# One transfer for a key tail, a weight half ahead of a read, and a new order in a fused linear-attention and expert kernel

## The chip, the cores and the metric

The kernel runs on one core of one Trainium2 chip. The metric is the device time of one execution in microseconds (us); the engines are TensorE (PE), VectorE (DVE), ScalarE (ACT), GpSimd (POOL) and the queue of SyncE (SP), which issues most transfers.

## The reference

For 8 batches of 8 heads, 576 tokens and 64 columns a head, linear attention is computed and normed, and its 4608 rows of 512 go to one of 16 experts each:

```
kv  = einsum('bhsd,bhse->bhde', k, v)
out = einsum('bhsd,bhde->bhse', q, kv)
x   = out / sqrt(mean(out*out) + 1e-6) * g_norm      # rows of 512
g   = argmax(x @ w_group);  e = argmax(x @ w_expert[g])
y   = softmax weight of g * softmax weight of e * (relu(x @ w1[g, e]) @ w2[g, e])
```

All data are float32. w1 is 512x1024 and w2 is 1024x512 for each expert.

## The kernel before

**Attention.** A batch b has four blocks of 128 tokens and a tail of 64; the tails of two batches (a pair `pb`) share one 128-row piece. So there are 36 tiles of 128 tokens. `load` (L481) brings the main blocks of q, k and v of a batch, 1024 KB each (those of k and v of batch 0 in two halves), and `load_tail` the tails. A tail of v or q is one transfer of 128 partitions (L499). The tail of k goes into `ktail`, a tile of two columns of 512: the rows of the first batch in partitions 0 to 63 of column 0, those of the second in partitions 64 to 127 of column 1, and zeros elsewhere (written once, L488). So k's tail takes two transfers of 64 partitions (L496). `kv_product` (L518) multiplies k and v in four steps of two heads; its fifth term is the tail. `kv_keep`, `kv_transpose`, `kvt_keep`, `router_product` and `router_keep` turn kv into `kvx`, which also holds the router's columns. `o_product` (L564) makes a tile's attention and router logits in one product; ACT copies them out (`o_keep` L569, `logits_keep`, which like the copies of kv is recorded at L507) and squares them (L585); DVE sums the squares (L592).

**Routing.** The tiles form eight groups (6, 5, 5, 4, 4, 5, 4 and 3 tiles). `route` works out each token's expert and row in some 25 small DVE and ACT steps, and POOL then writes each tile with one indirect transfer to `xs` (`put_rows`, L248). After group 1 the busiest expert is chosen (`pick`, which writes `star_idx`); after group 4 (`EARLY`) the place of its first 256 rows is known. When all puts of groups 0 to 4 have landed, `early_region` reads these rows (L273), and `early_weights` loads the expert's four weight halves of 1024 KB (L204), each step behind the one before, the first behind the read. `early_products` scales and transposes the rows (L283, L1182, L1187), multiplies by w1 (L329, eight steps `l1`; ACT's `hhi` L1205 and DVE's `hlo` L1211 behind each) and by w2 (L1234), while the last groups are still being routed.

**The planner.** All of this is a list of steps (engine, cost in us, rank, needs). `give_out` puts them into one written order for each engine: at each turn it takes, on the engine that can start earliest, the step that can start no later than all others of that engine, and among equals the one of lowest rank. "S" stands for the transfers as one resource, START is the time from which a resource is free, and `take` and `give` count 11 slots of a shared pool `big` in which loads and weight pieces live. RANK, ROUTE, FOLD, LOADS, QLOADS and KVS are offsets of the ranks. Idle time of PE in the plan is filled with products of constants (`fill`, tile `warm`, L412). The engines then run their lists in order.

**From the attention to the expert loop.** This stretch is written out by hand. Rows and weights of the second region (r = 0 is what remains of the same expert, r = 1 the next expert) are read; `split_high` (ACT, L227) and `split_low` (DVE, L231) split weights into a high and a low float32r part, and three products (`three`, lines 340, 341 and 345) replace one. The rest r = 0 runs w1 in two halves `hf`, each followed by ACT's relu into `hr` (L1503); `turn(hf)` transposes a half of `hr` on PE (L1475), copies it out on ACT (L1478) and subtracts on DVE (L1479) into `la`; `rest_layer2` needs both. Between them stand the preparations of r = 1: DVE transposes its rows in four pieces (`turned`, L291), ACT scales them (`split_high_x`, L1387) and DVE subtracts (`split_low_x`, L1391).

**The expert loop.** Regions 1 to 15, each layer 1 in eight steps `f` and layer 2 in four steps `d`. In r = 1 the first four steps f also carry one operation each of `quarter_masks` (L1526, L1529, L1531), which mark the rows that count; `indices(1)` follows at f = 4, and POOL scales the rows of r = 2 at f = 0 (L301).

Of the kernel before, what the change touches and what calls it, by code (L numbers as in the profile page):

```python
# [9 lines left out]
F32 = mybir.dt.float32  # L10
# [3 lines left out]
AF = mybir.ActivationFunctionType  # L14
# [21 lines left out]
RANK = {'hl': -4.24, 'wh': -7.85, 'wd': -2246.36, 'ek': 18.16, 'o': 21.14, 'ok': 46.15, 'sq': -11.92, 'red': 65.62, 'w': 51.39, 'wl': -3.08, 'wl2': -1661.94, 'xt': 52.95, 'xs': -122.49, 'l1': 20.45, 'hs': -22.88, 'l2': 25.69, 'lk': -5267.97}  # L36
ROUTE = [1124.11, -2951.7, 3842.35, -3791.13, 68.67, -44.77, -25.9, -5.46]
FOLD = [38.06, 8.5, 5073.95, 6.04, 11066.38, 26.92, -26.59, -20.62]
# [15 lines left out]
START = {"PE": 4.5, "A": 0.5, "D": 0.5, "G": 7.5, "S": 5.8, "R": 9.0, "W": 0.0}  # L54
BIG = 11
CUT = 3

@with_exitstack
def tile_linattn_moe(ctx: ExitStack, tc: tile.TileContext, qm, qt, k, v, router, w1, w2, out):
    nc = tc.nc  # L60
    P = 128
# [311 lines left out]
    with ExitStack() as ph:  # L373
# [96 lines left out]
        def get(*key):  # L470
            return done.get(key)
# [37 lines left out]
        def kv_product(b, pr):  # L509
            if pr == 0:  # L510
                kv["ps"] = ps_k.tile([P, 512], F32, name="kps", tag="psk")
            km, vm, kt, vt = raw["k", b], raw["v", b], tails["k", b // 2], tails["v", b // 2]
# [83 lines left out]
        def attention_steps():  # L596
            for b in range(B):
# [6 lines left out]
                for hi, hs in enumerate(hss):  # L604
                    for x, nm in enumerate(order[:2]):
                        done["load", b, nm, hi] = step(
                            "S", 2.6 / len(hss), f + LOADS[b] + 0.1 * x + 0.3 * hi, [get("load", b, nm, hi - 1)],
# [5 lines left out]
                done["load", b, "q", 0] = step("S", 2.6, f + QLOADS[b], [],  # L613
                                               lambda b=b: load("q", b, everything), take=1)
                if b % 2:
                    done["tail", "q", pb] = step("S", 0.65, f + QLOADS[b] + 0.1,
                                                 [get("o", NT * (pb - 2) + 2 * NJ)] if pb >= 2 else [],
                                                 lambda pb=pb: load_tail("q", pb))
                prev = get("kk", b - 1)
                for pr in range(NP):  # L620
# [3 lines left out]
                                                        done["tail", "k", pb], done["tail", "v", pb]],  # L624
# [6 lines left out]
                prev = step("PE", 0.62, f + RANK["ek"], [prev, get("ek", b - 1)], lambda b=b: kv_transpose(b))  # L631
# [25 lines left out]
        def route(g):  # L657
# [235 lines left out]
            for c in cols:  # L893
# [3 lines left out]
                step("S", 0.7, -100000.0, [prev], lambda: None)  # L897
# [236 lines left out]
        def early_weights():  # L1134
# [3 lines left out]
            for i in range(4):  # L1138
                (wv, rows, cols) = ((w1v, DM, FF // 2), (w2v, FF, DM // 2))[i // 2]

                def f(i=i, wv=wv, rows=rows, cols=cols):
                    if i == 0:
# [4 lines left out]
                               [wt[-1] if wt else st["read"], done["star_idx"]], f,  # L1147
# [129 lines left out]
    with ExitStack() as ph:  # L1277
# [207 lines left out]
        x1, xts = new_x(), []  # L1485
        for hf in range(2):
            ps = ps_h.tile([P, 512], F32, name="ps")
            for c in range(KC):
                if hf == 1 and c == 2:
                    for i in range(2):  # L1490
                        xts.append(turned(1, i))
                        split_high_x(x1[0], xts[i], 1, i)
                    split_low_x(x1, xts[0], 1, 0)
                    turn(0)
                    split_high(w1n[0], 0)
                    xts.append(turned(1, 2))
                    split_low_x(x1, xts[1], 1, 1)
                    split_high_x(x1[0], xts[2], 1, 2)
                    split_low(w1n[0], 0, nc.vector)
                    w1n.append(half_layer(ev, 0, 1))  # L1500
# [215 lines left out]
```

## Time and profile before

| what | value |
|---|---|
| median of 3 runs | 552.08 us (551.42 to 553.18) |
| the profiled execution | 551.76 us |
| its span, first to last instruction | 550.1 us |
| PE busy in the span | 533.0 us, 97% |
| DVE, ACT, POOL busy | 397.7, 281.1, 256.7 us |

The time of the profiled execution is 1.7 us more than its span. A busy PE is not a useful PE: the products of constants at L412 count as busy, so they are looked at apart.

### The profile page before, as it was taken

To read this page: it belongs to the slowest core of one execution; us is meant where nothing else is said; L and a number is where in the kernel's file an instruction comes from. 1 tells how busy PE (TensorE), PEld (TensorE's weight loads), DVE (VectorE), ACT (ScalarE), POOL (GpSimd) and SP (SyncE) were. 2 spreads that over 40 slices of the span, in tenths; PEclk is the share of its full clock that TensorE was granted. 3 is DMA by queue.
4 is the path that set the end of the run, shared out by engine and by line. 5 is a ranking of instruction groups with operands and counts; after the bars stand their busy time and mean duration, and the time that the engine had idled before them with its cause. 6 is when DMAs were issued, how large, how long until landed. Compare 5 with 4: busy or idle time off the path is not lost. (4 is left out here: it accounts for less than half of the span.)

```text
span 550.1 us, 11705 instructions
## 1 busy us (share of the span) xinstructions
PE 533.0 (97%) x4275; PEld 511.0 (93%) x4281; DVE 397.7 (72%) x844; ACT 281.1 (51%) x497; POOL 256.7 (47%) x272
## 2 busy tenths in 40 slices
PE   6999999899999999999999999999999999999995
PEld 3789988689899999999999999999999999999994
DVE  2248999689786786787768677777868777877750
ACT  0377887644653544445354454545453556555440
POOL 5000775452101644737383736455463737355261
PEclk9999999999999999999999999999999999999998
DMA  8999997958987374626756556564738374762010
GB/s 265 377 415 364 415 422 303 337 235 251 326 298 298 85 271 127 242 108 173 276 191 212 199 201 229 168 253 147 278 121 320 87 322 165 262 251 111 9 37 35
DMA packets 44463, 126.30 MB, mean 230 GB/s; under 512 B 6901, under 2 KB 26857, under 8 KB 33396
## 3 DMA queue, kind: packets, MB, share of 16 engines
q1 hardware_dynamic: 36468, 106.01, 53.6%
q0 software_dynamic: 7792, 19.48, 9.5%
q8 instruction: 34, 0.56, 0.4%
q10 hardware_dynamic: 144, 0.04, 0.1%
q14 instruction: 25, 0.20, 0.1%
HBM read 106.04 MB, written 20.58 MB: 230 GB/s over the span
## 5 line engine op out<-in xcount | busy, mean ns | idle before, releaser
L1395 POOL DMA_INDIRECT out_dram<-z,idx x141 | 167.8, 1190 | 169.7 <-DVE idx L1373 131.0
L340 PE MATMUL ps<-xh,whi 128*128 128x364 f32 (+14 forms) x480 | 143.8, 300 | 0.0
L341 PE MATMUL ps<-xl,whi 128*128 128x364 f32 (+14 forms) x480 | 143.8, 300 | 0.0
L345 PE MATMUL ps<-xh,wlo 128*128 128x364 f32 (+14 forms) x480 | 143.7, 299 | 0.0
L345 PE MATMUL psy<-hh,w2l 128*128 128x364 f32 (+13 forms) x448 | 135.0, 301 | 0.4 <-DVE w2l L318 0.4
L340 PE MATMUL psy<-hh,w2h 128*128 128x364 f32 (+13 forms) x448 | 135.1, 302 | 0.0
L341 PE MATMUL psy<-hl,w2h 128*128 128x364 f32 (+13 forms) x448 | 134.8, 301 | 0.0
L231 DVE TENSOR_TENSOR wlo<-wr,whi 128x1024 fp32r<-128x1024 f32 x64 | 94.9, 1486 | 23.2 <-ACT whi L227 23.2
L304 ACT ACTIVATE hh<-ps 128x364 fp32r<-128x364 f32 (+14 forms) x120 | 50.5, 421 | 81.6 <-PE ps L345 79.1
L345 PEld LDWEIGHTS ps<-xh,wlo 128*128 128x128 f32 x480 | 90.6, 189 | 0.0
L340 PEld LDWEIGHTS ps<-xh,whi 128*128 128x128 f32 x480 | 90.6, 189 | 0.0
L341 PEld LDWEIGHTS ps<-xl,whi 128*128 128x128 f32 x480 | 90.5, 188 | 0.0
L314 ACT CAST w2h<-wr 128x1024 fp32r<-128x1024 f32 x60 | 62.6, 1043 | 46.9 <-PE psy L341 46.9
L318 DVE TENSOR_TENSOR w2l<-wr,w2h 128x1024 fp32r<-128x1024 f32 x60 | 73.4, 1224 | 17.8 <-ACT w2h L314 17.3
L345 PEld LDWEIGHTS psy<-hh,w2l 128*128 128x128 f32 x448 | 84.5, 189 | 0.7 <-DVE w2l L318 0.7
L341 PEld LDWEIGHTS psy<-hl,w2h 128*128 128x128 f32 x448 | 84.7, 189 | 0.0
L340 PEld LDWEIGHTS psy<-hh,w2h 128*128 128x128 f32 x448 | 84.6, 189 | 0.0
L305 DVE SCALAR_TENSOR_TENSOR hl<-ps,hh 128x364 fp32r<-128x364 f32 (+14 forms) x120 | 55.7, 464 | 28.0 <-ACT hh L304 27.9
L248 POOL DMA_INDIRECT xs<-xo,keys x36 | 36.1, 1004 | 72.6 <-DVE ohs L756 47.3
L227 ACT CAST whi<-wr 128x1024 fp32r<-128x1024 f32 x64 | 66.4, 1037 | 2.3 <-DMA wr<-in_w_dram 2.3
L1387 ACT ACTIVATE xh<-xt,rw 128x364 fp32r<-128x364 f32 (+14 forms) x60 | 32.6, 545 | 67.6 <-DVE xt L291 67.6
L1597 DVE STREAM_TRANSPOSE z<-psy 128x320 f32<-128x320 f32 (+3 forms) x56 | 28.6, 510 | 23.0 <-PE psy L345 23.0
(289 smaller groups left out, 667.5 us busy)
## 6 DMA issues: line engine op xcount, KB each, us to landing
wr<-in_w_dram SPq DMA_DIRECT2D x64, 1024.0 KB
m_q<-in_qm_dram SPq DMA_DIRECT2D x8, 1024.0 KB
m_k<-in_k_dram SPq DMA_DIRECT2D x7, 1024.0 KB
m_v<-in_v_dram SPq DMA_DIRECT2D x7, 1024.0 KB
xq<-xs SPq DMA_DIRECT2D x24, 136.0 KB
xq<-xs SPq DMA_DIRECT2D x20, 153.0 KB
out_dram<-z,idx POOLq DMA_INDIRECT x141
xq<-xs SPq DMA_DIRECT2D x8, 187.0 KB
```

What stands on the lines that cost most here:

```text
L227: nc.scalar.copy(out=hi, in_=w)
L231: eng.tensor_tensor(out=lo, in0=w, in1=hi.bitcast(F32), op=ALU.subtract)
L248: sc = nc.gpsimd.indirect_dma_start(out=xs, out_offset=bass.IndirectOffsetOnAxis(ap=keys[:, c:c + 1], axis=0), in_=x.rearrange("p i f -> p ...
L304: nc.scalar.activation(out=hh, in_=ps, func=AF.Relu)
L305: nc.vector.scalar_tensor_tensor(out=hl, in0=ps, scalar=0.0, in1=hh.bitcast(F32), op0=ALU.max, op1=ALU.subtract)
L314: nc.scalar.copy(out=piece(hi, hf, i2), in_=halfpiece(wt[hf][0], i2))
L318: nc.vector.tensor_tensor(out=piece(lo, hf, i2), in0=halfpiece(wt[hf][0], i2), in1=piece(hi, hf, i2).bitcast(F32), op=ALU.subtract)
L340: nc.tensor.matmul(ps, lhsT=stat_h(c), rhs=mov_h(c), start=(c == 0), stop=False)
L341: nc.tensor.matmul(ps, lhsT=stat_h(c), rhs=mov_l(c), start=False, stop=False)
L345: nc.tensor.matmul(ps, lhsT=stat_l(d), rhs=mov_h(d), start=False, stop=(d == n - 1))
L1387: nc.scalar.activation(out=xh[:, c, 0:CAPS[r]], in_=xt[:, 0:CAPS[r]], func=AF.Copy, scale=g2[:, 0:1])
L1395: sc = nc.gpsimd.indirect_dma_start(out=out4, out_offset=bass.IndirectOffsetOnAxis(ap=idx[:, g:g + 1], axis=0), in_=z[:, g, :], in_offset= ...
```

## The change

The tail of k is loaded in one transfer of 128 partitions into a tile of its own, and a new step `place` copies each batch's 64 rows into `ktail` beside the zeros: on DVE for the first pair, on POOL for the second and third, on ACT for the last (`PLACE`). `kv_product` waits for its copy. The first half of the early weights needs only `star_idx`, and no longer the early read; the other halves wait for the read and for the half before. Ahead of the expert loop the turned first half of `hr` is copied before the scaled rows of r = 1, several preparations of r = 1 move behind the first piece of `rest_layer2`, and the four mask operations move there from the first steps of r = 1. Some of the planner's costs and all its ranks are new, so the order of steps on every engine up to the early products may differ. The diff, its tables and moves cut to their core:

```diff
-RANK = {'hl': -4.24, ... 'wl': -3.08, 'wl2': -1661.94, ...}
+RANK = {'hl': 25.95, ... 'wl': 2652.43, 'wl2': -2193.01, ...}
-LOADS = [-7192.68, -5292.19, -3785.25, -22.6, -13.29, 20.34, 66.64, 3836.81]
-QLOADS = [-4068.6, -19.7, -9.18, 21.75, 24.7, 15.01, 83.86, 8384.54]
-KVS = [578.35, -63.62, -20.16, 16.13, -4689.41, 25.21, -6.01, 18.47]
+LOADS = [-10174.1, -4595.36, -1584.83, -17.0, -6.34, 40.36, 37.95, 595.29]
+QLOADS = [-1724.83, -1249.21, -46.17, 25.23, 8.61, 32.6, 768.25, 3876.23]
+KVS = [69.45, -43.3, 766.59, 8.86, -57.74, -78.23, 39.83, 8872.18]
...
-START = {"PE": 4.5, "A": 0.5, "D": 0.5, "G": 7.5, "S": 5.8, "R": 9.0, "W": 0.0}
+START = {"PE": 4.5, "A": 0.5, "D": 0.5, "G": 7.5, "S": 2.9, "R": 9.0, "W": 0.0}
+PLACE = 'DGGA'
...
         def load_tail(nm, pb):
-            if nm == "k":
-                tails[nm, pb] = ktails[pb % 2]
-                for x in range(2):
-                    sl = slice(x * TAIL, (x + 1) * TAIL)
-                    nc.sync.dma_start(tails[nm, pb][sl, x, :], k[pb][sl, NJ])
-                return
             tails[nm, pb] = ap_.tile([P, H * D], F32, name=f"tail_{nm}")
             nc.sync.dma_start(tails[nm, pb], qt[pb].rearrange("p r s -> p (r s)") if nm == "q" else
-                              v[pb][:, NJ])
+                              {"k": k, "v": v}[nm][pb][:, NJ])
+
+        def place_tail(pb, x):
+            sl = slice(x * TAIL, (x + 1) * TAIL)
+            {"A": nc.scalar.copy, "D": nc.vector.tensor_copy, "G": nc.gpsimd.tensor_copy}[PLACE[pb]](
+                out=ktails[pb % 2][sl, x, :], in_=tails["k", pb][sl])
...
+                done["place", b] = step(PLACE[pb], {"A": 0.6, "D": 0.55, "G": 0.9}[PLACE[pb]], f + KVS[b] - 0.1,
+                                        [done["tail", "k", pb]] + [get("kv", b - 4, pr) for pr in range(NP) if b >= 4],
+                                        lambda pb=pb, x=b % 2: place_tail(pb, x))
...
-                                                        done["tail", "k", pb], done["tail", "v", pb]],
+                                                        done["place", b], done["tail", "v", pb]],
...
                 wt.append(step("S", 2.53, groups[EARLY][-1] + RANK["wl2" if i > 1 else "wl"] + 0.1 * i,
-                               [wt[-1] if wt else st["read"], done["star_idx"]], f,
+                               ([] if i == 0 else [wt[-1], st["read"]]) + [done["star_idx"]], f,
                                take=1))
...
                 if hf == 1 and c == 2:
+                    xts = [turned(1, i) for i in range(2)]
+                    turn(0)
                     for i in range(2):
-                        xts.append(turned(1, i))
                         split_high_x(x1[0], xts[i], 1, i)
                     split_low_x(x1, xts[0], 1, 0)
-                    turn(0)
-                    split_high(w1n[0], 0)
                     xts.append(turned(1, 2))
                     split_low_x(x1, xts[1], 1, 1)
-                    split_high_x(x1[0], xts[2], 1, 2)
-                    split_low(w1n[0], 0, nc.vector)
                     w1n.append(half_layer(ev, 0, 1))
...
         rest_layer2(0, 0, 4)
+        split_high(w1n[0], 0)
+        for _ in quarter_masks():
+            pass
         turn(1)
         xts.append(turned(1, 3))
-        split_low_x(x1, xts[2], 1, 2)
-        split_high_x(x1[0], xts[3], 1, 3)
+        for i in range(2, 4):
+            split_high_x(x1[0], xts[i], 1, i)
+        split_low(w1n[0], 0, nc.vector)
+        for i in range(2, 4):
+            split_low_x(x1, xts[i], 1, i)
         split_high(w1n[0], 1)
-        split_low_x(x1, xts[3], 1, 3)
         split_low(w1n[0], 1, nc.vector)
...
                 if r > 1:
                     next(tables, None)
                     next(tables, None)
-                elif f < 4:
-                    next(masks, None)
                 elif f == 4:
```

## Rows read from the trace of the kernel before

**Rows 1.** Busy time by stage: length, PE, PEld, DVE, ACT, POOL, PE clock, DMA share, GB/s

```profile
0.00:20.00 20.00, 14.52 (x139) 8.03 (x143) 4.84 (x16) 1.87 (x2) 7.37 (x47) 1.00 0.93 312
20.00:100.00 80.00, 78.00 (x1000) 70.29 (x999) 61.04 (x240) 62.17 (x154) 28.96 (x43) 1.00 0.96 373
100.00:147.00 47.00, 44.62 (x288) 38.33 (x288) 38.40 (x121) 23.77 (x44) 16.99 (x25) 1.00 0.84 290
147.00:533.20 386.20, 385.76 (x2792) 385.25 (x2791) 293.38 (x468) 191.97 (x295) 200.71 (x156) 1.00 0.56 197
```

**Rows 2.** The same for the products of constants (L412) alone, PE and PEld

```profile
0.00:20.00 20.00, 9.66 (x32) 3.71 (x34) 1.00 0.93 312
20.00:100.00 80.00, 3.68 (x13) 1.70 (x17) 1.00 0.96 373
```

**Rows 3.** What PE waited for, whole span: total us, times, longest us

```profile
PE kps L518 <- DMA m_v<-in_v_dram: 1.9, 2, 1.1
PE kps L518 <- DMA tail_v<-in_v_dram: 1.4, 2, 0.9
PE l L329 <- DMA wr<-in_w_dram: 1.0, 1, 1.0
...
PE ops L564 <- DMA m_q<-in_qm_dram: 0.5, 1, 0.5
PE psy L345 <- DVE w2l L318: 0.4, 1, 0.4
PE ps L340 <- ACT la L1478: 0.3, 1, 0.3
PE ps L345 <- DVE la L1479: 0.2, 1, 0.2
```

**Rows 4.** SP's timeline: start us, us, line, transfer, count

```profile
66.37 0.33 SPq L481 DMA_DIRECT2D m_q<-in_qm_dram  x1
...
96.11 0.40 SPq L273 DMA_DIRECT2D xq<-xs  x1
97.11 2.12 SPq L204 DMA_DIRECT2D wr<-in_w_dram  x4
```

**Rows 5.** POOL's timeline, the last put of group 4

```profile
91.54 1.14 POOL L248 DMA_INDIRECT xs<-xo,keys  x1 [0.30 <-issue]
```

**Rows 6.** Short stretches by engine, columns as in rows 1

```profile
22.00:23.00 1.00, 1.00 (x10) 0.98 (x8) 0.79 (x2) 0.00 (x0) 0.00 (x0) 1.00 1.04 434
24.00:25.00 1.00, 1.00 (x9) 0.77 (x7) 0.25 (x1) 0.97 (x4) 0.00 (x0) 1.00 0.98 209
25.00:26.00 1.00, 0.90 (x7) 0.90 (x7) 0.43 (x1) 1.00 (x4) 0.00 (x0) 1.00 1.07 252
94.00:97.00 3.00, 3.00 (x25) 2.66 (x24) 2.57 (x13) 2.44 (x6) 0.00 (x0) 1.00 0.02 6
```

**Rows 7.** PE's timeline where the early products begin; in brackets the idle time before

```profile
103.29 1.04 PE L412 MATMUL warm<-wide_b,ones_b 128*128 128x512 bf16 x4
105.31 0.89 PE L329 MATMUL l<-xx,wr 128*128 128x256 f32 x3 [0.98 <-DMA wr<-in_w_dram]
```

**Rows 8.** ACT's timeline there

```profile
104.56 0.43 ACT L507 COPY xr<-ops 128x160 f32<-128x160 f32 x1
109.04 0.38 ACT L1205 ACTIVATE hhi<-l 128x256 fp32r<-128x256 f32 x1 [4.06 <-PE l L329]
```

**Rows 9.** The issues of k's tails: duration ns min/median/max, first and last start us

```profile
L496 SPq DMA_DIRECT2D ktail<-in_k_dram x8: 471/472/586, 1.9 to 53.8; - x8
```

**Rows 10.** A copy of 128x512 on ACT, as in rows 9

```profile
L569 ACT COPY xo<-ops x36: 567/586/659, 23.5 to 103.4; 128x512 f32<-128x512 f32 x36
```

**Rows 11.** The first two mask operations on DVE, as in rows 9

```profile
L1526 DVE TENSOR_TENSOR badq<-wq,lohi x1: 2494/2494/2494, 150.2 to 150.2; 128x192 f32<-128x192 f32 x1
L1526 DVE TENSOR_TENSOR bad<-wq,lohi x1: 341/341/341, 154.2 to 154.2; 128x192 f32<-128x192 f32 x1
```

**Rows 12.** POOL's timeline at the same time

```profile
149.67 2.78 POOL L301 TENSOR_TENSOR xq<-xq 128x1536 f32<-128x1536 f32 x1 [0.84 <-DMA xq<-xs]
```

More of the change, by code (lines that the diff above doesn't have):

```diff
@@ L511, in kv_product @@
                 kv["ps"] = ps_k.tile([P, 512], F32, name="kps", tag="psk")
-            km, vm, kt, vt = raw["k", b], raw["v", b], tails["k", b // 2], tails["v", b // 2]
+            km, vm, kt, vt = raw["k", b], raw["v", b], ktails[b // 2 % 2], tails["v", b // 2]
             for j in range(NJ + 1):
@@ L606, in attention_steps @@
                         done["load", b, nm, hi] = step(
-                            "S", 2.6 / len(hss), f + LOADS[b] + 0.1 * x + 0.3 * hi, [get("load", b, nm, hi - 1)],
+                            "S", 2.7 / len(hss) if b == 0 else 2.55, f + LOADS[b] + 0.1 * x + 0.3 * hi, [get("load", b, nm, hi - 1)],
                             lambda nm=nm, b=b, hs=hs: load(nm, b, hs), take=1 if hi == 0 else 0)
@@ L612, in attention_steps @@
                                                         lambda nm=nm, pb=pb: load_tail(nm, pb))
-                done["load", b, "q", 0] = step("S", 2.6, f + QLOADS[b], [],
+                done["load", b, "q", 0] = step("S", 2.55, f + QLOADS[b], [],
                                                lambda b=b: load("q", b, everything), take=1)
@@ L896, in route @@
                 done["in", c] = do("W", 0, [prev], lambda: None, us=1.0)
-                step("S", 0.7, -100000.0, [prev], lambda: None)
+                step("S", 0.68, -100000.0, [prev], lambda: None)
             v["fold"] = False
@@ L1531, in quarter_masks @@
             nc.vector.tensor_scalar(out=badq, in0=badq, scalar1=FAR, scalar2=None, op0=ALU.mult)
-        masks = quarter_masks()
+        x1 = new_x()
+        for hf in range(2):
+            ps = ps_h.tile([P, 512], F32, name="ps")
+            for c in range(KC):
+                if hf == 1 and c == 2:
+                    xts = [turned(1, i) for i in range(2)]
+                    turn(0)
+                    for i in range(2):
+                        split_high_x(x1[0], xts[i], 1, i)
+                    split_low_x(x1, xts[0], 1, 0)
+                    xts.append(turned(1, 2))
+                    split_low_x(x1, xts[1], 1, 1)
+                    w1n.append(half_layer(ev, 0, 1))
+                three(ps, KC, lambda c: xT[:, c, :], lambda c: xTl[:, c, :], lambda c: w1r[hf][1][:, c, :],
+                      lambda c: w1r[hf][2][:, c, :], lo=c, hi=c + 1)
+            nc.scalar.activation(out=hr[:, hf * 512:(hf + 1) * 512], in_=ps, func=AF.Relu)
+        rest = [ps_h.tile([P, 512], F32, name="ps")[:, 0:DM // 2] for hf in range(2)]
+        w2n = [half_layer(ev, 1, 0)]
+        rest_layer2(0, 0, 4)
+        split_high(w1n[0], 0)
+        for _ in quarter_masks():
+            pass
+        turn(1)
+        xts.append(turned(1, 3))
+        for i in range(2, 4):
+            split_high_x(x1[0], xts[i], 1, i)
+        split_low(w1n[0], 0, nc.vector)
+        for i in range(2, 4):
+            split_low_x(x1, xts[i], 1, i)
+        split_high(w1n[0], 1)
+        split_low(w1n[0], 1, nc.vector)
+        w2n.append(half_layer(ev, 1, 1))
+        rest_layer2(1, 0, 4)
+        yo = mp.tile([P, DM], F32, name="yo")
+        for hf in range(2):
+            rest_layer2(hf, 4, FC)
+            nc.scalar.copy(out=yo[:, hf * (DM // 2):(hf + 1) * (DM // 2)], in_=rest[hf])
+        scatter_rows(yo, P, ridx[:, 0:1])
         cur, w1c, w2c = x1, w1n, w2n
```

36 lines of the change are left out of this document (4 added, 32 removed).

## The prediction

> **What bounds the kernel now.** I read first the busy time by stage. In the expert loop, from 147.0 to 533.2 us, PE is busy for 385.8 of 386.2 us [rows 1]: nothing there can be had except 0.4 us. What the change can move is the time at which the loop starts. Up to 147 us PE is not full: 5.5 us idle up to 20 us, 2.0 us from 20 to 100, 2.4 us from 100 to 147 [rows 1], and of what counts as busy 9.7 and 3.7 us are products of constants [rows 2]. Real slack from 20 us on is thus 2.0 + 3.7 + 2.4, some 8 us, a few of them products of constants between the early steps; the 15 us ahead of 20 us are the wait for the first data.
>
> Then the list of what PE waited for [rows 3]. Three kinds matter. Waits for k, v and q data, 1.9 + 1.4 + 0.5 us. One wait of 1.0 us for a weight half ahead of the early products. And 0.3 + 0.2 us for `la`, the turned values, with 0.4 us for `w2l` in the loop.
>
> Last, the transfers. They run at 93 and 96% of their share up to 100 us [rows 1], with one hole: from 94 to 97 us they move next to nothing, 6 GB/s [rows 6]. There SP stands in its list and waits until the puts of group 4 have landed; the last of them starts at 91.54 us [rows 5], the early read is issued at 96.11 us and the four weight halves from 97.11 us on [rows 4]. The first half is in place only when PE has stood for 0.98 us, at 105.31 us [rows 7]. ACT meanwhile stands for 4.06 us in front of `hhi` [rows 8], and with it the routing of the last two groups, which is queued behind.
>
> **The change, part by part.**
>
> **A. The first weight half ahead of the read.** It needs one slot and `star_idx`, known since group 1, so its step can be issued any time from some 66 us on; by its rank (23 + 2652) it comes after the loads of k and v of the last batch (31 + 595) but before the last q (31 + 3876). It is one transfer of 1024 KB (1.05 MB), 2.4 us at the 434 GB/s of an undisturbed slice [rows 6]. The hole of 3 us holds it. PE's wait of 0.98 us goes [rows 7]: the products can start when the products of constants end, 104.33 us. Upper bound 1.0 us, as PE has work up to there. Lower bound 0.2 us: ACT's copy of the router's columns ends at 104.99 us [rows 8], and if its buffer is the one that the first product writes, this wait is late next. I read the order of buffers as asking for the copy before that one, so I take **1.0 us**. The other three halves land 2.4 us sooner too, behind ample cover. SP gains nothing else: the transfer is issued by the same queue, in front of an instruction that waits anyway; behind it stand the last q and its tail, used by products that began at 93 us, and then the read.
>
> **B. The key tail in one transfer.** Four tails, each two transfers of 128 KB, 0.262 MB. In the slice in which such a pair runs the rate is 209 GB/s, in the next one, with v's tail of the same bytes in one transfer, 252, against 434 just before [rows 6]. One transfer in place of two takes 0.262 MB at 252 instead of 209 GB/s: 1.04 for 1.25 us, 0.2 us; at 434 it would be 0.60 us, a gain of 0.65 us. Only the first two tails lie where PE waits for data; later PE has its loads well ahead. So 0.4 to 1.3 us in transfers; nothing at all if the k and v blocks behind are late for another reason. SP issues four transfers fewer, 0.47 us each [rows 9], of which only the first counts, since later the queue is full anyway: 0 to 0.5 us. I take **0.6 us**, near the row of v's tail, which is the same shape.
>
> The Trainium skill, SBUF — State Buffer, section "Door 1: The DMA port swizzle", says that 64 partitions reach only half of the 16 ports, some 218 GB/s, and 128 reach all. The 209 GB/s agree with its first half; v's tail at 252 does not reach what the second would allow. By the page the gain would be the upper 1.3 us, and the sum below 0.7 us larger.
>
> The copies: eight of 64x512. No row shows one. ACT's 128x512 copy takes 0.59 us [rows 10]; POOL's 128x1536 operation takes 2.78 us [rows 12], a third of which is 0.93 us. Two on DVE at the start, where DVE is busy for 4.8 of 20 us [rows 1]: free, but kv of batch 0 now waits for tail, copy and perhaps the copy of batch 1, some 1.2 us after k's tail, about when v's tail lands. Four on POOL ahead of its first put, where it has nothing to do. Two on ACT, 1.2 us in a stage in which ACT is busy for 62 of 80 us: covered by 18 us of idle time. Net zero; without the cover 1.2 us for ACT's pair.
>
> **C. The order ahead of the loop.** The copy of the turned values no longer stands behind two scalings on ACT, and the subtraction no longer behind one of DVE's. Both PE waits, 0.3 + 0.2 us, go [rows 3]. Against it DVE gets four mask operations ahead of the second turn. In the loop the first took 2.49 us and the second 0.34 us for the same shape [rows 11]; the first ran while POOL scaled rows from 149.67 to 152.45 us [rows 12]. At the new place POOL is idle, so I count three at 0.34 us and a last one estimated at no more: 1.4 us at most. The second subtraction then ends about when PE wants it, after 24 matmuls and four transposes. Bounds: a loss of 0.5 us, a gain of 0.8 us. I take **0.5 us**. What is late next is the low part of the first weights of r = 1, which now comes after the masks and the second turn; by my count it is done under 1 us before PE asks.
>
> **D. The masks out of r = 1.** DVE loses 3.5 us in the first steps of the loop, and the wait of 0.4 us for `w2l` [rows 3] stood at the end of that queue: **0.4 us**, bounds 0 and 0.4.
>
> **E. The new order.** No row shows it. It can at best take the products of constants and idle time from 20 to 100 us, 5.7 us [rows 1, 2], and at worst put a wait like ACT's 4.06 us [rows 8] on PE's path. I take **0**, and let it widen the range by some 1.5 us on both sides.
>
> Sum: 1.0 + 0.6 + 0.5 + 0.4 = 2.5 us of the profiled 551.76 us, so 549.3 us. The median of the runs is 0.3 us higher; I keep 549.4 us.
>
> **The rivals.**
>
> *The wait changes hands.* The first early product waits for ACT's copy instead of the weights (A 0.2 us), PE's work after 30 us swallows what B brings, and the masks eat C. Left are 0.2 + 0.4 us: 551.3 us, no change. For it speaks that ACT's copy ends only 0.3 us before the product starts [rows 7, 8], and that PE and the transfers are both nearly full from 20 to 100 us [rows 1]; against it that PE's named wait is the transfer's. 25%.
>
> *The planner finds more.* If the new order also takes half of the 5.7 us of E, the time is 551.8 - 2.5 - 2.8 = 546.5 us. For it speaks that there is such slack; against it that the loads then have to come earlier too, and they run at 96%. 12%.
>
> *A copy in a queue holds PE (slower).* ACT and POOL run their lists in order. If ACT's copy of the last tail stands behind an instruction that itself waits for PE, kv of batch 6 waits for it, and all of PE's list behind it. The price is a wait such as the 4.06 us in front of `hhi` [rows 8] and the copy's 0.6 us; less the 2.5 us of the sum, 551.8 + 2.2 = 554.0 us. It decides once kv of a batch starts over 4.1 us after its data have landed (2.5 us for the sum and the bound of 1.6). Against it: the tails land far ahead of kv from 30 us on. 10%.
>
> *The early half is in the way.* Issued at 66 us, into full queues, its 2.4 us could push back the last q and the puts, and with them the read. The early products then start at 104.3 + 2.4, 1.4 us later than now; with B, C and D the end is as before, 551.7 us. The hole of 3 us speaks against a full push. It shares the 25% of the first rival. That the change does not do what it says, with the half still issued behind the read, would leave 1.5 us of the sum, 550.3 us; the rank and the missing need make it unlikely, and it lies within the range.
>
> **How the numbers follow.** A measurement of this kernel can tell 0.3% from no change, 1.7 us: faster is below 550.4, slower above 553.7 us. The forecast, 549.4 us, has 53%, and its own range by the bounds of A to D is 548.1 to 551.6 us; I count 52 of the 53 below 550.4. With the larger gain (12%) this makes 64% for faster, 26% for the same and 10% for slower. The range for 8 in 10 takes in the rival without change and most of the larger gain: 546.8 to 552.3 us.
>
> **What would show it.** In the profile after: the first of L204 ahead of L273 on SP, and bytes in the hole around 95 us. L329 without a wait for `wr`, starting about 1.5 us earlier than 105.31 (A and B together). No slice near 209 GB/s at the tails. No PE wait for `la` and for `w2l`; masks at 0.34 us each ahead of the loop. The loop's first L340 at about 144.7 us and its length unchanged. The forecast is wrong if PE's list shows new waits between 30 and 100 us, or if L329 starts as late as before with another name behind its wait.

## The result and the profile after

The changed kernel takes **545.51 us** (median of 4 runs, 545.30 to 545.87), the kernel before 552.38 us in the same job (551.42 to 553.18): ratio 0.9897, 95% interval 0.9868 to 0.9925, so 6.9 us faster. Forecast were 549.4 us and a range from 546.8 us. The direction was right, the size was not. The profiled execution took 545.87 us, span 544.2 us, against 551.76 and 550.1 us.

One remark on all that follows: in the jobs of e5 and of e11 to e18 TensorE's instructions came with gaps of half a microsecond from some 58 us on, the expert loop was 15 to 28 us longer, and the kernel before itself took 594.7 to 596.9 us, so these runs are set against the kernel before of their own job and read in detail only up to 57 us.

The busy time by stage of the changed kernel, with the columns of [rows 1], the loop now from 141 us on:

```profile
0.00:20.00 20.00, 14.25 (x194) 8.96 (x196) 5.73 (x20) 1.87 (x2) 7.18 (x46) 1.00 0.91 336
20.00:100.00 80.00, 76.89 (x955) 70.34 (x960) 62.52 (x248) 61.95 (x162) 30.45 (x48) 1.00 0.98 399
100.00:147.00 47.00, 46.95 (x300) 42.46 (x299) 40.53 (x122) 24.74 (x44) 18.39 (x26) 1.00 0.75 249
```

From 20 to 100 us the transfers move 399 GB/s where they moved 373. From 100 us on PE is almost without a gap. Single microseconds around the second key tail, then the hole in the transfers ahead of the read, and the place where it was before:

```profile
24.00:25.00 1.00, 1.00 (x9) 1.00 (x8) 0.94 (x3) 0.50 (x3) 0.00 (x0) 1.00 1.07 418
25.00:26.00 1.00, 1.00 (x8) 0.96 (x8) 0.21 (x1) 1.00 (x3) 0.40 (x1) 1.00 1.01 406
...
92.00:94.00 2.00, 2.00 (x16) 1.91 (x14) 2.00 (x4) 1.85 (x6) 0.00 (x0) 1.00 0.10 25
94.00:97.00 3.00, 2.47 (x28) 1.84 (x28) 2.86 (x16) 2.12 (x8) 0.00 (x0) 1.00 0.96 349
```

The slices with 209 and 252 GB/s [rows 6] run at 418 and 406, **both** of them, and no microsecond from 20 to 30 us is under 373: v's tail, which the change does not touch, lies in that stretch too. The hole ahead of the read is not filled. It has moved with the read, to 92 to 94 us with 25 GB/s, and the bytes at 94 to 97 us are those of the three weight halves behind the read. The list of SP and then of PE, where the early products begin, where the stretch ahead of the loop begins and where the loop begins:

```profile
58.67 0.35 SPq L205 DMA_DIRECT2D wr<-in_w_dram  x1
...
92.83 0.40 SPq L274 DMA_DIRECT2D xq<-xs  x1
93.51 1.94 SPq L205 DMA_DIRECT2D wr<-in_w_dram  x3
```

```profile
100.81 5.34 PE L330 MATMUL l<-xx,wr 128*128 128x256 f32 x24
...
128.98 0.39 PE L341 MATMUL ps<-lc,lb 128*128 128x512 f32 x1
...
141.09 0.33 PE L341 MATMUL ps<-xh,whi 128*128 128x364 f32 x1
```

Before, these five points were: read issued 96.11 [rows 4], early products 105.31 [rows 7], stretch ahead of the loop 133.43, loop 147.01, end 550.1 us, the third and fourth by these rows of PE:

```profile
133.43 0.39 PE L340 MATMUL ps<-lc,lb 128*128 128x512 f32 x1
...
147.01 0.33 PE L340 MATMUL ps<-xh,whi 128*128 128x364 f32 x1
```

The loop starts 5.92 us sooner, and that divides into four:

| from | to | before, us | after, us | difference |
|---|---|---|---|---|
| start | read issued | 96.11 | 92.83 | -3.28 |
| read issued | early products | 9.20 | 7.98 | -1.22 |
| early products | stretch ahead of the loop | 28.12 | 28.17 | +0.05 |
| that stretch | loop's first matmul | 13.58 | 12.11 | -1.47 |
| loop | end | 403.09 | 403.11 | +0.02 |

The first two rows of the table cannot be taken apart. A second profile of the kernel before (e19) has the read later and the early products at the same time as the first, without any wait for `wr`:

```profile
97.45 0.40 SPq L273 DMA_DIRECT2D xq<-xs  x1
```

```profile
105.44 5.34 PE L329 MATMUL l<-xx,wr 128*128 128x256 f32 x24
```

In e6, with the same steps up to there, the two are at 97.09 and 105.42 us, with a wait for `wr` of 0.2 us. What holds in all three is the sum: the early products start 4.5 to 4.6 us sooner in the changed kernel.

What PE waited for in the changed kernel (compare [rows 3]):

```profile
PE kps L518 <- DMA m_v<-in_v_dram: 3.7, 4, 1.9
...
PE kps L518 <- DVE ktail L499: 0.9, 1, 0.9
PE ops L564 <- DMA m_q<-in_qm_dram: 0.8, 1, 0.8
PE psy L346 <- DVE w2l L319: 0.4, 1, 0.4
```

The waits for `wr` and `la` are gone; that for `w2l` in the loop stands at 0.4 us as before. The copy for the first pair holds PE for 0.9 us, and PE waits longer for v than before: a list of waits, summed, would call this kernel's first 100 us worse. The start of the early products says otherwise.

### The profile page after: what moved, and what is told of

Its sections match the earlier page's. It is cut to its first block, busy times and chain, and to the rows that moved or that the text cites. A ratio compares the mean times of both kernels' runs of the same rounds, so it can differ in the third digit from the quotient of the medians.

```text
span 544.2 us, 11700 instructions
## 1 busy us (share of the span) xinstructions
PE 528.3 (97%) x4266; PEld 510.5 (94%) x4272; DVE 398.4 (73%) x846; ACT 277.7 (51%) x499; POOL 256.7 (47%) x276
## 5 line engine op out<-in xcount | busy, mean ns | idle before, releaser
L319 DVE TENSOR_TENSOR w2l<-wr,w2h 128x1024 fp32r<-128x1024 f32 x60 | 75.5, 1258 | 18.0 <-ACT w2h L315 17.6
```

What stands on the lines that cost most here:

```text
L319: nc.vector.tensor_tensor(out=piece(lo, hf, i2), in0=halfpiece(wt[hf][0], i2), in1=piece(hi, hf, i2).bitcast(F32), op=ALU.subtract)
```

## The experiments

Two theories. **T**: the key tails' transfers of 64 partitions are slow themselves and slow what stands behind them; their width is most of the gain. **O**: the new written order is most of it, and the tails are small as forecast. Later a third, **J**: the wide tails pay only in an order found for them.

**e1: the tails in two halves of 64 partitions again**, copies and written order as in the changed kernel.

```diff
+            if nm == "k":
+                for x in range(2):
+                    sl = slice(x * TAIL, (x + 1) * TAIL)
+                    nc.sync.dma_start(tails[nm, pb][sl], k[pb][sl, NJ])
+                return
```

> The changed kernel, with each tail of k again in two transfers of 64 partitions, into the same tile; copies, ranks and written order as they are. Theory T (the transfers): the slow stretch around each tail, v's tail included, comes from the two half-width transfers, and their removal is most of the 3.3 us by which the early read moved. Then slices of about 200 to 260 GB/s come back at the first three tails, the read is issued 1.5 to 3 us later than 92.8 us and the time rises by 1.5 to 3 us, to 547 to 548.5. Theory O (the order): the 3.3 us come from the order found anew, so the time rises by at most 0.6 us, to 546.1, even if the slow slices come back.

Measured: 551.24 us, 0.9983 of the kernel before (0.9962 to 1.0005). With this one edit 5.7 of the 6.9 us are gone. Short stretches of e1, columns as in [rows 1], then its waits:

```profile
24.00:25.00 1.00, 1.00 (x11) 1.00 (x9) 0.00 (x0) 1.00 (x4) 0.00 (x0) 1.00 1.02 258
25.00:26.00 1.00, 1.00 (x10) 1.00 (x10) 0.84 (x2) 1.00 (x4) 0.00 (x0) 1.00 1.03 242
...
62.00:64.00 2.00, 0.86 (x28) 0.86 (x30) 1.42 (x5) 0.56 (x3) 1.44 (x4) 1.00 1.01 420
64.00:66.00 2.00, 2.00 (x47) 2.00 (x44) 1.97 (x6) 0.00 (x0) 1.72 (x3) 0.54 1.04 432
66.00:68.00 2.00, 2.00 (x22) 1.88 (x21) 0.20 (x1) 0.73 (x2) 1.72 (x5) 0.61 1.02 409
```

```profile
PE kps L523 <- DMA m_v<-in_v_dram: 5.1, 5, 2.2
...
PE kps L523 <- POOL ktail L504: 1.9, 2, 1.1
PE kps L523 <- DVE ktail L504: 1.3, 1, 1.3
```

The slow slices are back, v's among them. The read is issued at 97.98 us, 5.15 us later than with the wide transfer; the stretch and the loop are as in the changed kernel (12.12 us, 402.7 us). All of the loss lies ahead of the early products, which start at 106.83 us, 6.0 us later. The lists of PE, ACT, DVE and POOL are the same in both kernels, instruction by instruction, so ACT's n-th output copy in one can be set against the n-th in the other. The seventeenth, first in the changed kernel, then in e1:

```profile
55.47 0.58 ACT L569 COPY xo<-ops 128x512 f32<-128x512 f32 x1 [0.38 <-PE ops L564]
```

```profile
59.66 0.59 ACT L574 COPY xo<-ops 128x512 f32<-128x512 f32 x1 [0.38 <-PE ops L569]
```

The first copy is 1.9 us later in e1 (23.24 for 21.39), the fifth, behind the second pair's tails, 3.2 (33.77 for 30.61), the seventeenth, behind the third pair's, 4.2, and the last, at 102 us, 6.0. So the delay grows at each of the first three pairs and is not caught up.

The loss is more than theory T asked for, and the rows of this one run show one reason: with v late PE stood for 2.2 us up to 63.1 us, and in the 4 us from 64 us on its granted clock was 0.54 and 0.61, near the lower level of 1.2 GHz. It can't be the main one: runs of e1 with a mean granted clock of 0.999 took 549.30 and 551.43 us. Theory O falls for this order: with narrow tails it gives nothing that can be measured, although e1 still has the early half and the new stretch.

**e2: two transfers again, but of 128 partitions and half the columns each**, so the same bytes and the same count as in e1.

```diff
+            if nm == "k":
+                for x in range(2):
+                    sl = slice(x * H * D // 2, (x + 1) * H * D // 2)
+                    nc.sync.dma_start(tails[nm, pb][:, sl], k[pb][:, NJ, sl])
+                return
```

> The changed kernel, with each tail of k in two transfers of the same 128 KB, but each of all 128 partitions and half of the columns. Theory W (the width): what is slow is a transfer that reaches only half of the partitions, so this kernel shows no slice under 330 GB/s at the tails and runs like the changed one, 545.5 us within 0.6. Theory N (the number): what is slow is the small transfer or one more of them, so it is as slow as with split rows, within 0.6 us of that kernel.

Measured: 545.74 us (ratio 0.9890, 0.9854 to 0.9927), as the changed kernel. Short stretches of e2:

```profile
24.00:25.00 1.00, 1.00 (x9) 1.00 (x9) 0.91 (x4) 0.70 (x2) 0.00 (x0) 1.00 1.11 419
25.00:26.00 1.00, 1.00 (x10) 1.00 (x9) 0.42 (x1) 0.80 (x3) 0.13 (x1) 1.00 1.08 434
```

Neither the number of transfers nor their issues nor the 128 KB of each cost anything that can be seen: the width does. Why it does, the runs do not show, and it does not in every place. The fourth pair of the kernel before goes out in halves too, from 51.27 us on, and is multiplied from 74.36 us on; between 51 and 74 us no microsecond is under 393 GB/s, and together they run at 417:

```profile
51.00:74.00 23.00, 22.70 (x243) 20.84 (x244) 21.30 (x84) 19.59 (x51) 14.40 (x24) 1.00 1.02 417
```

What spares the fourth pair stays open. The 0.5 us that the prediction allowed for fewer issues is not there.

**e3: the early half behind the read again** (part A undone).

```diff
-([] if i == 0 else [wt[-1], st["read"]]) + [done["star_idx"]], f,
+[wt[-1] if wt else st["read"], done["star_idx"]], f,
```

> The changed kernel, with the first weight half again behind the early read. If the prediction's part A holds (1.0 us, of which the two traces show 1.2 us between read and first early product), the first early product waits for the weights again by 1 us or more and the time rises by 1.0 to 1.5 us, to 546.5 to 547. Rival: the planner writes another order around it and the wait is hidden elsewhere: less than 0.4 us.

Measured: 546.25 us (ratio 0.9901, 0.9864 to 0.9938), 0.7 us more than the changed kernel; the loop starts at 141.55 instead of 141.09 us. The order shifts a little (read at 91.31 us, early products at 100.58), and waits of 1.2 and 0.7 us for ACT come up in place of the one for `wr`. Part A is worth 0.5 to 0.7 us, below the 1.0 to 1.5 us that were expected.

**e4: the old stretch ahead of the loop, masks in the loop** (C and D undone).

> The changed kernel, with the stretch ahead of the expert loop as it was, masks in the first steps of the loop again. The traces show this stretch 1.5 us shorter, so the time rises by 1.5 us, to 547. Rival, the prediction's part C: 0.5 us, the rest of the 1.5 being due to an earlier arrival of rows and weights, to 546.0. The loop's length does not change, as the two traces show.

Measured: 546.83 us (ratio 0.9909, 0.9879 to 0.9940), 1.3 us more. The stretch takes 13.40 us again, the loop to the end 402.85 us.

**e6: the kernel before with the new stretch and the masks ahead of the loop** (C and D alone).

> The kernel before with the new stretch ahead of the expert loop and the masks in it, nothing else. If the 1.3 us that the changed kernel loses with the old stretch belong to the stretch alone: 1.0 to 1.5 us less than before, about 551. Rival: rows or weights arrive too late for it in the old order, less than 0.5 us.

Measured: 550.48 us against 552.14 us (ratio 0.9968, 0.9946 to 0.9990), 1.7 us less; the stretch takes 12.24 us, the loop to the end 403.63 us. Both directions agree on 1.3 to 1.7 us for C with D, and in every kernel that was built the stretch is 13.2 to 13.6 us in the old form and 12.1 to 12.3 us in the new one, 12.1 us in e5 and e15 too, which leave the masks in the loop. Where that comes from is seen in PE's list of the kernel **before**, at the turned values:

```profile
139.18 0.40 PE L345 MATMUL ps<-la,lb 128*128 128x512 f32 x1
139.92 0.39 PE L340 MATMUL ps<-whi,la 128*128 128x256 f32 x1 [0.34 <-ACT la L1478]
140.15 0.28 PE L341 MATMUL ps<-wlo,la 128*128 128x256 f32 x1
140.65 0.39 PE L345 MATMUL ps<-whi,la 128*128 128x256 f32 x1 [0.22 <-DVE la L1479]
...
141.81 0.28 PE L345 MATMUL ps<-whi,la 128*128 128x256 f32 x1
142.25 0.66 PE L1475 MATMUL ps<-ident,hr 128*128 128x128 f32 x4 [0.16 <-ACT hr L1503]
```

and in the changed kernel's:

```profile
134.68 0.39 PE L346 MATMUL ps<-la,lb 128*128 128x512 f32 x1
134.91 0.28 PE L341 MATMUL ps<-whi,la 128*128 128x256 f32 x1
135.03 0.28 PE L342 MATMUL ps<-wlo,la 128*128 128x256 f32 x1
```

The brackets say 0.34, 0.22 and 0.16 us. But the matmuls overlap: undisturbed one starts 0.23 us after a 128x512 and 0.12 us after a 128x256. From start to start the three waits cost 139.92 - 139.18 - 0.23 = 0.51, 140.65 - 140.15 - 0.12 = 0.38, and 142.25 - 141.81 - 0.12 = 0.32 us, together 1.2 us. The bracket counts idle time only from the end of the matmul before, and leaves out the overlap that is lost each time.

**e5 and e15: the changed kernel with the masks back in the loop** (D alone), run twice.

> The changed kernel with the four mask operations of DVE back in the loop's first expert. If moving them gave nothing (loop's length was 403.1 us in both): 545.1 to 545.9 us, the first mask operation takes about 2.5 us beside POOL's scaling again and the w2l operation after it falls from 3.15 to about 1.2 us. If the move was worth the 0.4 us that was forecast: 545.9 to 546.4 us, with the loop longer by 0.4 us.

> The changed kernel with the four mask operations of DVE back in the loop's first expert (a first run fell on the same chip). If moving them gave nothing: 545.1 to 545.9 us, the first mask operation takes about 2.5 us beside POOL's scaling again and the w2l operation after it falls from 3.15 to about 1.2 us. If the move was worth the 0.4 us that was forecast: 545.9 to 546.4 us, with the loop longer by 0.4 us.

Measured: 590.89 and 590.96 us, 0.9961 and 0.9956 of the kernel before in the same jobs (0.9914 to 1.0009, 0.9880 to 1.0032). Such runs cannot tell 0.4 us. Of their rows one missed: the first mask took 0.35 us, ahead of POOL's scaling and not beside it. It was the second mask that ran beside it and took 2.50 us in both runs, and the first `w2l` behind it fell to 1.21 us. What is left on D are the loops of the other runs: 402.5 to 403.4 us with the masks in it (before, e4, e7, e9, e19), 402.7 to 403.6 without (after, e1, e2, e3, e6, e10). D gave nothing that shows beside such a spread. In the changed kernel DVE's list reads:

```profile
136.42 0.35 DVE L1493 TENSOR_TENSOR badq<-wq,lohi 128x192 f32<-128x192 f32 x1
...
146.74 3.15 DVE L319 TENSOR_TENSOR w2l<-wr,w2h 128x1024 fp32r<-128x1024 f32 x1 [0.32 <-ACT w2h L315]
150.74 1.23 DVE L319 TENSOR_TENSOR w2l<-wr,w2h 128x1024 fp32r<-128x1024 f32 x1
```

The masks are cheap at their new place, but POOL's scaling (146.02 to 148.80 us) now falls on the first `w2l`, which takes 3.15 instead of 1.23 us. The 2.2 us that the first mask lost before [rows 11, 12] were not the mask's: whatever DVE did beside that scaling paid them. But this is not why D gave nothing. The `w2l` that PE waits for comes later, and DVE stood idle for 0.40 us ahead of it until ACT had written `w2h`, in the kernel before and in the changed one:

```profile
162.66 1.23 DVE L318 TENSOR_TENSOR w2l<-wr,w2h 128x1024 fp32r<-128x1024 f32 x1 [0.40 <-ACT w2h L314]
```

```profile
156.74 1.23 DVE L319 TENSOR_TENSOR w2l<-wr,w2h 128x1024 fp32r<-128x1024 f32 x1 [0.40 <-ACT w2h L315]
```

The masks did not stand in its way, so taking them out could not bring it forward.

**e7: the kernel before with the wide tails and copies as planned steps, old ranks.**

> The kernel before, with k's tail in one transfer and the copies beside the zeros; ranks, costs, early weights and the stretch ahead of the loop as before. Theory T (the transfers are worth most of the gain by themselves): the slow slices cost some 4 us of transfers by 50 us, PE waits for data only up to some 32 us, so 2 to 4 us less than before, 548.5 to 550.5 us. Theory J (joint: the transfers give time that only the new order can use): less than 1.5 us, 551 to 552.4.

Measured: **559.66 us**, 1.0144 of the kernel before (1.0096 to 1.0193): 7.5 us slower, a miss for both theories. The transfers are fast (413 GB/s from 20 to 50 us, where the kernel before moves 373), and the output copies are 3.3 to 3.4 us ahead from the fifth (30.41 for 33.67 us) to the seventeenth (55.64 for 59.05). But with other steps in its graph the planner writes another order: from 80 to 100 us the transfers are down to 0.48 of their share, group 4's puts come late, the read is issued at 98.59 us, and behind it PE waits for ACT in the middle of the early products. Its longest wait:

```profile
PE l L1237 <- ACT hhi L1208: 4.6, 2, 3.1
```

**e9: the kernel before with the new ranks and costs, nothing else.**

> The kernel before, with the new ranks and costs of the planner alone. Theory O (the order): 2 us or more faster, 550.5 us or less. Theories T and J: no gain, within 1.5 us of before or slower, since the order counts on transfers that this kernel's tails make late, as split rows in the changed kernel do.

Measured: 554.02 us (ratio 1.0031, 1.0010 to 1.0051), 1.9 us slower. PE waits 3.4 and 2.5 us for v and its tail, and 1.7 us for `perm`, a wait that the kernel before does not have.

**e10: the changed kernel with the old ranks and costs.**

> The changed kernel with the ranks and costs of before: one transfer per tail, the early half's freedom and the new stretch, in the old order. Theory T: 546 to 547.5 us, the order being worth 2 us at most. Theories J and O: 548 us or more, since without the new order the transfers' time is not used.

Measured: 552.27 us (ratio 1.0012, 0.9993 to 1.0031): wide tails, early half and new stretch, and all of the gain gone. Read at 95.13 us, early products at 103.46, new waits of 1.3, 0.9 and 0.9 us for `xx`, `hhi` and `perm`. So e7, e9 and e10 say the same: ranks fit one graph, and any of these kernels whose order is worked out anew from ranks of another one loses 2 to 8 us. They can't say what the wide transfer is worth, since each moved the order as well.

**e11, e13, e16, e18: the wide tails in the kernel before, its written order kept.** The three first tails come in one transfer inside the same planned step, with the copies issued there; PE's and ACT's lists stay the same, instruction by instruction, DVE and POOL get the copies in addition. The fourth tail stays as it was.

```diff
+            if nm == "k" and pb < 3:
+                tails[nm, pb] = ktails[pb % 2]
+                t = ap_.tile([P, H * D], F32, name="tail_k")
+                nc.sync.dma_start(t, k[pb][:, NJ])
+                for x in range(2):
+                    sl = slice(x * TAIL, (x + 1) * TAIL)
+                    (nc.vector if pb == 0 else nc.gpsimd).tensor_copy(out=ktails[pb % 2][sl, x, :], in_=t[sl])
+                return
```

> The kernel before with its written order on all engines unchanged (TensorE's and ScalarE's lists are the same instruction by instruction); only the key tails of the first three pairs come in one transfer of 128 partitions and are copied beside the zeros by DVE (first pair) and POOL (second and third). The fourth pair keeps its two transfers of 64 partitions. Theory T (the half-width transfers alone carry the gain, whatever the order): the slow slices at 6 to 9, 23 to 27 and 42 to 46 us go, the read is issued 2 to 4 us earlier, 548.0 to 550.0 us. Theory J (the bytes come earlier, but the old order does not use them; the gain comes only with an order found for them): the slow slices go, the transfers of the first 60 us end 2 us or more earlier, but the read moves by less than 1 us, 551.2 to 552.6 us. A second slow result (over 554) would say that one transfer with copies is worse by itself.

> The kernel before with its written order unchanged on all engines; only the key tails of the first three pairs come in one transfer of 128 partitions and are copied beside the zeros by DVE (first pair) and POOL (second and third). A first run of it, on a chip that held TensorE at half clock for part of the attention stage, showed no slow slice and the last tail transfer issued at 64.9 us where the kernel before had 70.0 us. Theory T (the half-width transfers alone carry the gain, whatever the order): the read is issued 2 to 4 us earlier than 96.1 us, 548.0 to 550.0 us. Theory J (the old order does not use the earlier bytes): the read moves by less than 1 us, 551.2 to 552.6 us.

> The kernel before with its written order unchanged on all engines; only the key tails of the first three pairs come in one transfer of 128 partitions and are copied beside the zeros by DVE (first pair) and POOL (second and third). Two earlier runs fell on chips on which the kernel before took 596 us and TensorE's instructions came with gaps in the attention stage; up to there the transfers were 4 to 5 us ahead. Theory T (the half-width transfers alone carry the gain, whatever the order): the read is issued 2 to 4 us earlier than 96.1 us, 548.0 to 550.0 us. Theory J (the old order does not use the earlier bytes): the read moves by less than 1 us, 551.2 to 552.6 us.

> The kernel before with its written order unchanged on all engines; only the key tails of the first three pairs come in one transfer of 128 partitions and are copied beside the zeros. In three earlier runs, on chips where the kernel before took 595 to 597 us, ScalarE's copies of the outputs ran 1.1 to 1.8 us ahead of the kernel before at the first and 2.5 to 3.2 us at the seventeenth (56 us), then TensorE's instructions came with gaps. On a chip without these gaps theory T expects that lead to last to the read (93 to 94 us instead of 96.1) and 548.5 to 550.0 us; theory J expects it to be lost before the read, 551.2 to 552.6 us.

Measured: 586.86, 588.82, 591.95 and 589.20 us, 0.9882 (0.9824 to 0.9940), 0.9773 (0.9619 to 0.9926), 1.0051 (0.9955 to 1.0147) and 0.9888 (0.9812 to 0.9963) of the kernel before in the same jobs. Three are faster and one is not; that does not measure 3 us. But since the lists are the same, ACT's n-th output copy can be set against the n-th of the kernel before. First the kernel before, then e11:

```profile
23.47 0.58 ACT L569 COPY xo<-ops 128x512 f32<-128x512 f32 x1 [6.12 <-PE ops L564]
...
59.05 0.58 ACT L569 COPY xo<-ops 128x512 f32<-128x512 f32 x1 [0.31 <-PE ops L564]
```

```profile
56.11 0.58 ACT L577 COPY xo<-ops 128x512 f32<-128x512 f32 x1 [0.31 <-PE ops L572]
59.46 0.58 ACT L577 COPY xo<-ops 128x512 f32<-128x512 f32 x1 [1.56 <-remote]
```

The first copy is 1.1 to 1.8 us ahead in the four runs, that after the second pair's tails 2.4 to 3.1, the seventeenth 2.5 to 3.3 us (56.11 instead of 59.05 in e11). The last tail of q is issued at 64.9 us instead of 69.98. Then the gaps in PE's instructions begin, in all four at the same place, as this wait of e11 shows:

```profile
PE kps L526 <- issue: 6.6, 18, 0.5
```

So theory J is wrong in its strong form: the old order does use the earlier bytes, up to 57 us; e7, a run without the gaps, has the same lead there. Whether it lasts to the read and the end in the old order was not seen in an undisturbed job and stays open. In the new order it lasts, as e1 shows.

**e12, e14, e17: the same with the new stretch.**

> The same with the new stretch ahead of the loop (turned copy first, masks there) as well. If the two add up: the time of the run with the tails alone less 1.3 to 1.7 us. By theory T 546.5 to 548.5 us, by theory J 549.6 to 551.2 us.

> The same with the new stretch ahead of the loop as well (a first run fell on the same chip). If the two add up: the time of the run with the tails alone less 1.3 to 1.7 us; by theory T 546.5 to 548.5 us, by theory J 549.6 to 551.2 us.

> The same with the new stretch ahead of the loop as well. If the two add up: the time of the run with the tails alone less 1.3 to 1.7 us; by theory T 546.5 to 548.5 us, by theory J 549.6 to 551.2 us.

Measured: 593.38, 589.47 and 589.38 us, 0.9932 (0.9876 to 0.9988) and 0.9868 (0.9775 to 0.9961) of the kernel before for the first two, no ratio for the third. Inconclusive: whether the parts add up cannot be told from them.

**e19: the kernel before itself once more.**

> The kernel before itself, profiled on a chip of the later kind (where it takes some 596 us), so that the runs with the wide tails in the old order can be set against it on equal terms. If those chips differ only in the gaps of TensorE's instructions: its transfers and its first seventeen output copies come at the times of the first profile (23.5 us the first, 59.0 the seventeenth, within 0.5 us), so the lead of 2.5 to 3.2 us stands, and the gaps begin near 60 us in it too. If the lead at 56 us were the chip's doing, its copies would be some 3 us earlier than in the first profile as well.

Measured: 552.1 us. It met a job without the gaps, so it does not put the other four on equal terms. It does give the spread of the early copies: first at 23.98, seventeenth at 60.08 us, half a microsecond and one microsecond later than in the first profile. The lead of e11 and its repeats is thus 2.5 to 4.3 us against the two profiles of the kernel before, and not one of its four runs is as late as either.

## Why the prediction was wrong

**B, the step that failed.** The prediction priced the tails at 0.6 us and chose, between v's tail at 252 GB/s and the undisturbed 434, the row of v's tail, "which is the same shape". That row was no price of a wide transfer; it was an after-effect of the narrow pair queued just ahead. Without the pair the two slices at 24 and 25 us run at 418 and 406 GB/s (after), 419 and 434 (e2), and with it at 258 and 242 again (e1). So the cost of a pair has to be read from all slow microseconds, not from that of the pair. Over 6 to 9, 23 to 27 and 42 to 46 us the kernel before moves 698, 1096 and 1137 (GB/s times us), the changed one 1095, 1650 and 1623; at the changed rates the difference is 1.1 + 1.3 + 1.2 = 3.6 us of transfers in three of the four tails, where the prediction allowed at most 0.65 us a tail and 1.3 us in all. The fourth shows no such stretch. Between e1 and the changed kernel, which have the same order, the same sum is 3.3 us (767, 1145 and 1150 in e1), and what it costs in time is 5.7 us. The second sentence that failed with it is that only the first two tails count because PE has its loads well ahead later. In the old order it holds up to 57 us: e11's lead is 2.8 us ahead of the third pair and 2.9 behind it. In the new one it does not: e1 loses 1.0 us more at the third pair, and another 1.8 where PE waits 2.2 us for v up to 63 us.

The Trainium skill, SBUF — State Buffer, section "Door 1: The DMA port swizzle", which gives 64 partitions half of the ports, would have led to the larger price. For the first three pairs the trace agrees with it: e1's halves of 64 partitions bring 258 GB/s, e2's of 128 partitions 419 with the same bytes. For the fourth it does not, at 393 GB/s and more. The prediction saw the rule and set it aside for one row that only seemed to contradict it; but even its larger price, 1.3 us, is little over a third of the 3.6 us, because it priced the pair's own bytes and not the slow microseconds around them.

**A**: 1.0 us forecast, 0.5 to 0.7 us at the end (e3). The half stands ahead of the read and the wait for `wr` is gone, but the mechanism was not the one named. The half was issued at 58.67 us and did not go into the hole. The wait for `wr` was no fixed price either: 0.98 us in the profile that the prediction read, 0.2 in e6 and none in e19, with the early products at 105.3 to 105.4 us in all three. And in e3, without A, they start at 100.58 us, 0.2 us sooner than with it. e3 loses behind them, where PE waits 0.7 us for ACT's `xx`: 28.85 instead of 28.17 us up to the stretch.

**C**: 0.5 us forecast, 1.3 to 1.7 measured. The mechanism was right, the term was mis-sized: it took the idle time in the brackets of two waits. Start to start they cost 0.9 us, and a third wait, for `hr`, 0.3 us more.

**D**: 0.4 us forecast, nothing measured. The prediction put the wait for `w2l` at the end of DVE's queue behind the masks; but DVE stood idle for 0.40 us ahead of that operation, until ACT had written `w2h`. The 2.2 us lost beside POOL's scaling went from the mask to another `w2l`.

**E**: 0 with 1.5 us either way. This term has no value of its own. The new ranks alone cost 1.9 us (e9), without them the other parts give nothing (e10); with narrow tails the new order has its early products at 106.83 us, later than the old one with 105.31 (e1). The new order gains nothing without the wide tails (e1, e9), and the wide tails gain nothing in an order made anew from the old ranks (e7, e10). Most of what the prediction called "the planner finds more", 546.5 us with 12%, happened, but for a reason that it did not give: the loads did come earlier, as that rival demanded, and the prediction's own argument against it, that they run at 96% of their share, was misread: a share of 0.98 with 209 GB/s [rows 6] is time in which the engines are occupied, not bytes.

**The signs named ahead**: no slice near 209 GB/s, the half ahead of the read, no wait for `la` and `wr`, cheap masks and an unchanged loop are all there. Bytes around 95 us are there too, but not as a sign of A: the hole has moved to 92 to 94 us. The early products come 4.5 instead of 1.5 us sooner, the loop at 141.1 instead of 144.7 us, and the wait for `w2l` did not go. The slower rival did not show: ACT's copies of the last tail hold nothing, and what does hold PE, DVE's copy at the start, costs 0.9 us.

What stays open is how the 4.5 us ahead of the early products divide between wide tails and new order. In the old order the tails alone give about 3 us at 57 us (e11); in the new one taking them away costs 5.7 us (e1), in the profiled run some of it as half clock. Both put the tails well above A, C and D. But taking the new ranks away costs 6.8 us (e10), so the two cannot be added up: 5.7 and 6.8 together are more than the 6.9 us that there were to lose.

## What to carry to other kernels

A busy share of the DMA engines near 1 says nothing on the bytes: look at GB/s by microsecond, and price a slow transfer by all slow slices around it, those of its neighbours in the queue too. A wait read from one profile may be gone in the next while the work behind it starts no sooner, so read it in a second profile before you price it. Ask what the late operation itself waited for: an engine that stood idle ahead of it was not held by its queue. Price a wait in a stream of matmuls from start to start against the undisturbed pitch; the idle time shown is only part of it. And where ranks steer a planner, a single edit tried with ranks of another graph tests the order, not the edit; put the edit inside an existing step, so that the written order stays, before judging it.

## What the runs showed of the hardware that was not expected

- In three of four places a pair of transfers of 64 partitions (128 KB each) held down the rate for 3 to 4 us, to 203 to 342 GB/s, and the full-width transfer behind it with it; two transfers of the same bytes with 128 partitions left it at 350 to 434 in the same stretches (e2). In the fourth place the rate stayed at 393 GB/s and more (before, 51 to 74 us).
- Whichever DVE operation ran beside POOL's scaling of rows paid for it: 2.49 instead of 0.34 us for a mask [rows 11], 3.15 instead of 1.23 us for `w2l` in the changed kernel, 2.50 us for the second mask in e5 and e15.
- After PE had stood for 2.2 us, up to 63.1 us, its granted clock was 0.54 and 0.61 from 64 to 68 us (e1), close to the lower level, although PE was busy throughout these 4 us.
